# FFT plus mixture of experts on one core: the PSUM bank of the small sums becomes a second buffer for the second matmul's sums

## The chip, the cores and the metric

One core of a Trainium2 chip runs the whole kernel in one launch. The metric is the device time of that core in microseconds (us); lower is better. Three runs of the kernel before took 1113.00, 1111.27 and 1106.92 us, median 1111.27.

## The reference

```
X = np.fft.fft(x, axis=1)          # x: [8, 2496, 256] float32
X = np.fft.fft(X, axis=2)
t = X.real.reshape(19968, 256)
logits = t @ w_gate                # [256, 8]
e_idx  = argmax(logits);  gate_w = softmax(logits)[e_idx]
eom    = sigmoid(t @ w_output_gate)
h  = relu(t[rows of e] @ w1[e])    # w1: [8, 256, 1024]
ye = h @ w2[e]                     # w2: [8, 1024, 256]
out[rows of e] = gate_w * eom[:, e] * ye
```

Every one of the 19,968 tokens goes through one expert of eight, and which one is known only once its batch has been transformed.

## The kernel before, in words

**Transform.** The 8 batches are transformed one after another, in five steps each (`steps()`). `dstage` is the DFT along the features (its sums in a buffer of two PSUM banks, `psb_t`), `devac` splits its result into fp16 high and low parts (`ahi` on ACT, `alo` on DVE), `sstage` is the DFT along the sequence (again a `psb_t`), and `sevac` makes the finished rows. `gating` picks each token's expert on DVE, counts the tokens of each expert by two small matmuls (L592, L593) and has POOL scatter the rows to `scr` in device memory, sorted by expert.

**Experts.** The experts work on slots of 256 tokens. In each of three early rounds (as soon as 2, 4 and 6 batches are in `scr`) each expert gets two slots; a last round takes what is left after batch 8. `mm1` (L1134 on, its matmuls at L1146) makes 12 matmuls for one of a slot's four `hp` tiles (one PSUM bank each), ACT and DVE turn that into `hh` (L1150) and `hl` (L1151); `mm2` (matmuls at L1166) sums all four into one `yp` tile, which two ACT instructions scale into `y` (L1173, one for each 128 tokens), and POOL scatters `y` to the output.

**Weights.** SP loads the fp32 weights of an expert as four raw tiles (two halves of `w1`: `raw0b_134` and `raw0b_135`, two of `w2`: `raw1b_136` and `raw1b_137`), one buffer for each. In the first round a raw tile is first squared on ACT (`wsq`, L1107), which sums its energy; a matmul with ones adds that over the partitions (`wscale`, L369), and DVE makes a power of two of it (`p_w`, L276). ACT then converts the raw tile into an fp16 high part (`w0b` or `w1b`, L1126), DVE makes the low part (L1127), and only then can SP load the next expert's raw tile into that buffer (issued at L1095).

**Order.** `experts()` is the foreground and the transform steps of later batches are its background: the main loop takes one piece of the one, then as many of the other as its rates say. The order on SP and POOL is the order in which the program is written; on PE, ACT and DVE a scheduler picks it from the program and its buffers.

**PSUM.** There are eight banks. While early rounds and transform run together they hold two `hp`, one `yp`, two `psb_t` of two banks each, and one bank `psm_t` for all the small sums: the token counts (L592, L593), the energy of a batch (L455) and the weight energies (L369). From the last round on (pool `fpe2`) there are three `hp` and two `yp`. The pools of the first phase open again at the step FSTART, about 130 to 150 us into the span.

Of the kernel before, what the change touches and what calls it, by code (L numbers as in the profile page):

```python
# [11 lines left out]
F32 = mybir.dt.float32  # L12
# [221 lines left out]
def fft_moe_kernel(ctx: ExitStack, tc: tile.TileContext, xl, wg, w1, w2, tde, tdo, gt, ts0, tsm, tsr, tsq, cst, tid, out):  # L234
    nc = tc.nc
    PS = bass.MemoryType.PSUM
# [45 lines left out]
    if True:  # L282
        lp, xp, rp = ExitStack(), ExitStack(), ExitStack()
        pl = lambda st_, **kw: st_.enter_context(tc.tile_pool(reuse_waits="tile", **kw))
# [7 lines left out]
        pps = ExitStack()  # L292
        psb = pl(pps, name="psb", bufs=3, space=PS)
        psm = pl(pps, name="psm", bufs=2, space=PS)
        pool = {"b": psb, "m": psm}
# [59 lines left out]
        gate = {}  # L355
        smalls = {}

        def small():
            if "t" not in smalls:
                smalls["t"] = pool["m"].tile([128, 512], F32, name="psm_t", tag="m")  # L360
            return smalls["t"]

        wsrc = (w1, w2)
        wen = kp.tile([128, E, 2, 2], F32, name="wen")

        def wscale(e, m):
            ps = pool["m"].tile([128, 512], F32, name="psm_t", tag="m")[:, 0:1]
            for h in range(2):
                nc.tensor.matmul(ps, c_["ones"], wen[:, e, m, h:h + 1], start=(h == 0), stop=(h == 1))  # L369
            pow2_scale(pg, ps, 1, (7.0, 14.0)[m], "w", to=(wsc[:, m, e:e + 1], wiv[:, m, e:e + 1]))  # L370
            if m:
                nc.vector.tensor_mul(wsc[:, 2, e:e + 1], wiv[:, 0, e:e + 1], wiv[:, 1, e:e + 1])
# [180 lines left out]
        def gating(b):  # L553
# [11 lines left out]
            def t3(name, shape=(128, 20, 8)):  # L565
                return pg.tile(list(shape), F32, name="r_" + name, tag="r_" + name, bufs=1)

            m = t3("m", (128, 20))
# [19 lines left out]
            nc.vector.tensor_tensor_scan(inc.rearrange("p e j -> p (e j)"), c_["scanm"][P], oh.rearrange("p e j -> p (e j)"), 0.0, op0=ALU.mult, op1=ALU.add)  # L588
            yield
            yield "A"  # L590
            ps = pool["m"].tile([128, 512], F32, name="psm_t", tag="m")
            nc.tensor.matmul(ps[P, 0:8], c_["tri"][P], inc[:, :, 19], start=True, stop=True)  # L592
            nc.tensor.matmul(ps[:, 8:16], c_["ones"][P], inc[:, :, 19], start=True, stop=True)  # L593
            yield "C"
# [17 lines left out]
            t = t3("t", (128, 8, 20))  # L612
# [398 lines left out]
    if True:  # L1011
        fx = []
        psf = {}
# [51 lines left out]
        def scale_of(n, m):  # L1065
            rd, qi = sched[n][:2]
            return wsc[:, m, qi:qi + 1] if rd < LAST else ssc[:, m, qi:qi + 1] if rd == LAST else fbs[:, m, 0:1]
# [62 lines left out]
        def halves(a, h):  # L1130
            for k in ("hh", "hl"):
                a[k, h] = fx[0].tile([128, 4, 256], F16, name=k, tag=k, bufs=3)

        def mm1(n, g):  # L1134
            a = sl_[n]
            T = slice(0, a["N"])
            if g % 2 == 0:
                halves(a, g // 2)
            w1v = wbuf[a["wb"]][0][g // 2].rearrange("p a (k f) -> p a k f", k=2)
            ps = psf["h"].tile([128, 2, 256], F32, name="hp", tag="h", bufs=psf["hb"])  # L1140
            for k in range(2):
                f = 2 * g + k
                m = 0
                for kc in range(2):
                    for hl, x in ((0, kc), (0, 2 + kc), (1, kc)):
                        nc.tensor.matmul(ps[:, k, T], w1v[:, hl, kc, (f % 4) * 128:(f % 4 + 1) * 128], a["x"][:, x, T], start=(m == 0), stop=(m == 5))  # L1146
                        m += 1
            G = slice(2 * (g % 2), 2 * (g % 2) + 2)
            hh, hl = a["hh", g // 2], a["hl", g // 2]
            nc.scalar.activation(hh[:, G, T], ps[:, :, T], AF.Relu)  # L1150
            nc.vector.scalar_tensor_tensor(hl[:, G, T], ps[:, :, T], 0.0, hh[:, G, T], op0=ALU.max, op1=ALU.subtract)  # L1151

        def mm2(n, g):
            a = sl_[n]
            U, h = a["U"], g // 2
            M = min(128, a["N"])
            w2v = wbuf[a["wb"]][1][h].rearrange("p a (f d) -> p a f d", f=4)
            if g == 0:
                a["yp"] = psf["h"].tile([128, 2, 256], F32, name="yp", tag="y", bufs=psf["yb"])
                a["y"] = fx[0].tile([128, 2, 256], F32, name="y", tag="y", bufs=2)  # L1160
                a["ys"] = fx[0].tile([128, 2], F32, name="ysc", tag="ysc", bufs=2)
            u = g % 2 if U == 2 else 0
            for f in range(4) if U == 2 else range(2 * (g % 2), 2 * (g % 2) + 2):
                for m, (k, hl) in enumerate((("hh", 0), ("hh", 1), ("hl", 0))):

                    nc.tensor.matmul(a["yp"][0:M, u], a[k, h][:, f, u * 128:u * 128 + M], w2v[:, hl, f],  # L1166
                                     start=(g == 0 and f == 0 and m == 0), stop=(h == 1 and f == 3 and m == 2), skip_group_check=U == 2)
            ys = a["ys"]
            if g == 2:
                nc.vector.tensor_scalar(ys[:, 0:U], a["f"][:, 0:U, 0], scale_of(n, 2), None, op0=ALU.mult)  # L1170
            if g == 3:
                for u in range(U):
                    nc.scalar.activation(a["y"][0:M, u], a["yp"][0:M, u], AF.Copy, scale=ys[0:M, u:u + 1])  # L1173
                    put = nc.gpsimd.indirect_dma_start(  # L1174
                        out=out[:, :], out_offset=bass.IndirectOffsetOnAxis(ap=a["f"].bitcast(I32)[0:M, u, 1:2], axis=0),
                        in_=a["y"][0:M, u], in_offset=None, bounds_check=NTOK - 1, oob_is_err=False)
                    if sched[n][0] < FB:
                        free_order("out", put)
                del sl_[n]
# [114 lines left out]
    def background():  # L1294

        for m in steps_:
            yield C_STEP.get(m[0], C_END)
            if m[0] == "step":
                i, n = divmod(m[1], 5)
                for k, b in enumerate(BAS):  # L1300
                    if k and m[1] == 5 * b + 4:
                        for _ in table_a(k):
                            yield C_TAB
                    if m[1] == 5 * b + MARGIN:
                        ready.add(k)

                    if k and m[1] == 5 * b + 6 and k not in begun:
                        early(k, nc.sync.dma_start(fence, scr[DUM:DUM + 1, 0:1]))
        xp.close()
        for fill in (lambda: None, pads):  # L1310
            fill()
            while deferred:
                deferred.pop(0)()
                yield C_SCAT
        for _ in table_b():
            yield C_TAB
        pps.close()
        lp.close()
        fx.append(pl(ctx, name="fr2", bufs=2))
        psf["h"] = pl(ctx, name="fpe2", bufs=1, space=PS)  # L1320
        psf.update(hb=3, yb=2)
        add_raw(fx[1])
        add_wbuf(fx[1])
        ready.add(LAST)
# [9 lines left out]
    with tc.manual_schedule(engines=PH1):  # L1334
# [8 lines left out]
                break  # L1343
        pps.close()
        pps = ExitStack()
        psf["h"] = pl(ctx, name="fpe", bufs=1, space=PS)
        psf.update(hb=2, yb=1)
        pool["b"] = pl(pps, name="psb2", bufs=2, space=PS)
        pool["m"] = pl(pps, name="psm2", bufs=1, space=PS)
        next(fg)  # L1350
        load_x()
        bg = background()
# [44 lines left out]
```

## Time and profile before

| | |
|---|---|
| runs | 1113.00, 1111.27, 1106.92 us; median 1111.27 |
| profiled execution | 1110.9 us, its span 1109.0 us |
| granted TensorE clock, mean | 0.983 |
| PE busy | 1037.2 us, 94% of the span |
| ACT, DVE, POOL busy | 54%, 59%, 39% |
| matmuls recorded | 9866 |

The rows come from the trace of that one execution. A row of a timeline gives the start in us from the start of the span, the busy time, the engine, the line of the kernel, the operation, output<-inputs, the tile shapes, and how many like instructions stand in a row (x12); in square brackets is the idle time ahead of it and what ended that. A row of the waits says which instruction waited for which, how long in total, how many times, and the longest. A row of the chain is a piece of the chain of work that ended last. Names lack the buffer numbers in the trace and have them in the listings of the order.

### The profile page before, as it was taken

To read this page: it belongs to the slowest core of one execution; us is meant where nothing else is said; L and a number is where in the kernel's file an instruction comes from. 1 tells how busy PE (TensorE), PEld (TensorE's weight loads), DVE (VectorE), ACT (ScalarE), POOL (GpSimd) and SP (SyncE) were. 2 spreads that over 40 slices of the span, in tenths; PEclk is the share of its full clock that TensorE was granted. 3 is DMA by queue.
4 is the path that set the end of the run, shared out by engine and by line. 5 is a ranking of instruction groups with operands and counts; after the bars stand their busy time and mean duration, and the time that the engine had idled before them with its cause. 6 is when DMAs were issued, how large, how long until landed. Compare 5 with 4: busy or idle time off the path is not lost.

```text
span 1109.0 us, 27215 instructions
## 1 busy us (share of the span) xinstructions
PE 1037.2 (94%) x9866; PEld 928.0 (84%) x9866; DVE 654.5 (59%) x1352; ACT 599.6 (54%) x1095; POOL 434.5 (39%) x394
## 2 busy tenths in 40 slices
PE   5786679989899999999999999999999999999997
PEld 4675559878788999999998888888999989998996
DVE  6978646585577567557559454545355563555542
ACT  3765547665667456556554554554455553555542
POOL 0218835652675473346255772222221112212122
PEclk9998889999999999999999999999999999999999
DMA  9803465654546436466464786446556465665631
GB/s 353 308 19 115 151 171 153 180 166 130 157 133 194 123 104 167 119 158 164 137 166 122 204 208 171 144 105 181 135 138 183 127 183 133 156 180 144 170 87 28
DMA packets 152309, 170.97 MB, mean 154 GB/s; under 512 B 115309, under 2 KB 116207, under 8 KB 152164
## 3 DMA queue, kind: packets, MB, share of 16 engines
q1 hardware_dynamic: 136292, 126.48, 42.1%
q0 software_dynamic: 15728, 42.14, 11.4%
q8 instruction: 79, 1.29, 0.5%
q10 hardware_dynamic: 144, 0.52, 0.2%
q14 instruction: 66, 0.54, 0.2%
HBM read 149.51 MB, written 43.63 MB: 174 GB/s over the span
## 4 chain that ended last, share of the span: by engine, by line
PE 68%; DMA 11%; DVE 8%; ACT 5%; issue 4%; POOL 3%; SPq 1%; DVEq 0%; POOLq 0%; ACTq 0%
PE hp L1146 31%; PE yp L1166 30%; PE psb_t L516 4%; DMA raw1b<-in_w_dram 3%; DMA raw0b<-in_w_dram 3%; DMA out_dram<-y,xf 3%; PE psb_t L477 2%; DVE w0b L1127 2%; POOL scr L652 1%; ACT w1b L1126 1%; DMA scr<-rows,desti 1%; DVE w1b L1127 1%; POOL xt L408 1%; ACT w0b L1126 1%; ACT wsq L1107 1%
## 5 line engine op out<-in xcount | busy, mean ns | idle before, releaser
L1146 PE MATMUL hp<-xr,w0b 128*128 128x256 f16 (+2 forms) x4080 | 476.3, 267 | 10.5 <-DVE hl L1151 7.3
L1166 PE MATMUL yp<-w1b,hh 128*128 128x256 f16 x2560 | 437.6, 273 | 7.4 <-ACT y L1173 7.4
L1146 PEld LDWEIGHTS <-w0b 128*128 128x128 f16 x4080 | 381.1, 98 | 55.7 <-issue 8.2
L1174 POOL DMA_INDIRECT out_dram<-y,xf x160 | 187.4, 1171 | 542.4 <-ACT y L1173 501.8
L1166 PE MATMUL yp<-w1b,hl 128*128 128x256 f16 x1280 | 348.9, 273 | 0.0
L1151 DVE SCALAR_TENSOR_TENSOR hl<-hp,hh 128x512 f16<-128x512 f32 (+2 forms) x340 | 220.8, 654 | 204.5 <-ACT hh L1150 180.1
L1150 ACT ACTIVATE hh<-hp 128x512 f16<-128x512 f32 (+2 forms) x340 | 191.4, 566 | 234.9 <-PE hp L1146 231.1
L1166 PEld LDWEIGHTS <-hh 128*128 128x128 f16 x2560 | 248.6, 98 | 35.9 <-issue 8.2
L652 POOL DMA_INDIRECT scr<-rows,desti x160 | 174.3, 1089 | 76.8 <-issue 72.6
L1166 PEld LDWEIGHTS <-hl 128*128 128x128 f16 x1280 | 125.3, 98 | 14.4
L1173 ACT ACTIVATE y<-yp,ysc 128x256 f32<-128x256 f32 (+1 forms) x160 | 67.5, 469 | 45.0 <-PE yp L1166 40.4
L1127 DVE SCALAR_TENSOR_TENSOR w0b<-raw0b,wsc,w0b 128x1024 f16<-128x1024 f32 x44 | 60.7, 1379 | 49.4 <-ACT w0b L1126 49.4
L1127 DVE SCALAR_TENSOR_TENSOR w1b<-raw1b,wsc,w1b 128x1024 f16<-128x1024 f32 x44 | 56.3, 1281 | 42.4 <-ACT w1b L1126 41.6
L477 PE MATMUL psb_t<-tdet,ft 128*125 128x290 f32 (+1 forms) x200 | 61.1, 459 | 18.3 <-DVE ft L435 5.4
L477 PEld LDWEIGHTS psb_t<-tdet,ft 128*125 128x125 f32 (+1 forms) x200 | 40.7, 212 | 31.8 <-issue 9.6
L1126 ACT ACTIVATE w0b<-raw0b,wsc 128x1024 f16<-128x1024 f32 x44 | 50.3, 1145 | 30.2 <-PE hp L1146 29.2
L408 POOL TENSOR_TENSOR xt<-xt 128x500 f32<-128x500 f32 (+1 forms) x30 | 39.6, 1326 | 46.9 <-DMA xt<-in_xl_dram 32.9
L1126 ACT ACTIVATE w1b<-raw1b,wsc 128x1024 f16<-128x1024 f32 x44 | 50.3, 1145 | 13.0 <-PE yp L1166 13.0
L1127 DVE SCALAR_TENSOR_TENSOR w0b<-raw0b,ssc,w0b 128x1024 f16<-128x1024 f32 x32 | 40.8, 1282 | 22.5 <-ACT w0b L1126 21.6
L1127 DVE SCALAR_TENSOR_TENSOR w1b<-raw1b,ssc,w1b 128x1024 f16<-128x1024 f32 x32 | 41.1, 1283 | 21.9 <-ACT w1b L1126 21.0
L516 PE MATMUL psb_t<-ahi,tstq 125*128 125x145 f16 (+1 forms) x384 | 42.4, 229 | 2.2 <-DVE alo L490 2.2
L1126 ACT ACTIVATE w0b<-raw0b,ssc 128x1024 f16<-128x1024 f32 x32 | 36.3, 1144 | 14.7 <-DMA raw0b<-in_w_dram 13.6
(207 smaller groups left out, 950.8 us busy)
## 6 DMA issues: line engine op xcount, KB each, us to landing
raw0b<-in_w_dram SPq DMA_DIRECT2D x118, 512.0 KB
raw1b<-in_w_dram SPq DMA_DIRECT2D x118, 512.0 KB
xt<-in_xl_dram SPq DMA_DIRECT2D x40, 512.0 KB
scr<-rows,desti POOLq DMA_INDIRECT x160, 3.9
out_dram<-y,xf POOLq DMA_INDIRECT x160, 3.2
xr<-scr SPq DMA_TRANSPOSE x85
xf<-scr SPq DMA_DIRECT2D x75, 2.0 KB
tst<-in_ts_dram SPq DMA_DIRECT2D x2, 512.0 KB
```

Source lines behind the costliest of these rows:

```text
L408: eng.tensor_tensor(x0, x0, x1, op=ALU.add)
L477: nc.tensor.matmul(o[:, 0:290], ft[:, k, par, W], tdab[:, k], start=(k == 0), stop=(k == 1))
L516: nc.tensor.matmul(ps[:, k, c0:c0 + 145], tab[hl][t][K], a[K, kc, par, c0:c0 + 145], start=(n == 0), stop=(n == len(terms) - 1))
L652: free_order("scr", batch=b, inst=nc.gpsimd.indirect_dma_start(out=scr[:, :], out_offset=bass.IndirectOffsetOnAxis(ap=desti[:, j:j + 1], a ...
L1126: nc.scalar.activation(w[:, 0], r, AF.Copy, scale=sc)
L1127: nc.vector.scalar_tensor_tensor(w[:, 1], r, sc, w[:, 0], op0=ALU.mult, op1=ALU.subtract)
L1146: nc.tensor.matmul(ps[:, k, T], w1v[:, hl, kc, (f % 4) * 128:(f % 4 + 1) * 128], a["x"][:, x, T], start=(m == 0), stop=(m == 5))
L1150: nc.scalar.activation(hh[:, G, T], ps[:, :, T], AF.Relu)
L1151: nc.vector.scalar_tensor_tensor(hl[:, G, T], ps[:, :, T], 0.0, hh[:, G, T], op0=ALU.max, op1=ALU.subtract)
L1166: nc.tensor.matmul(a["yp"][0:M, u], a[k, h][:, f, u * 128:u * 128 + M], w2v[:, hl, f], start=(g == 0 and f == 0 and m == 0), stop=(h == 1 ...
L1173: nc.scalar.activation(a["y"][0:M, u], a["yp"][0:M, u], AF.Copy, scale=ys[0:M, u:u + 1])
L1174: put = nc.gpsimd.indirect_dma_start(out=out[:, :], out_offset=bass.IndirectOffsetOnAxis(ap=a["f"].bitcast(I32)[0:M, u, 1:2], axis=0), in_ ...
```

## The change

The early pools are laid out anew. `yp` gets a pool of its own with two banks (`fpy`), opened with the early rounds and kept to the end; `hp` keeps two banks, then three. There is no pool for the small sums any more (`pool["m"] = None`): the new function `few()` gives a small sum one bank of a `psb_t` buffer, of which there are two. So the 24 small-sum tiles made after the step FSTART (6 of the token counts, 4 of the batch energies, 14 of the weight energies) stand in line with `dstage` and `sstage` for those two buffers. No arithmetic is added or taken away. Every line from 358 on is numbered five higher in the changed kernel.

```diff
+        def few():
+            if pool["m"] is None:
+                return pool["b"].tile([128, 2, 512], F32, name="psb_t", tag="b")[:, 0]
+            return pool["m"].tile([128, 512], F32, name="psm_t", tag="m")
+
         def small():
             if "t" not in smalls:
-                smalls["t"] = pool["m"].tile([128, 512], F32, name="psm_t", tag="m")
+                smalls["t"] = few()
             return smalls["t"]
...
         def wscale(e, m):
-            ps = pool["m"].tile([128, 512], F32, name="psm_t", tag="m")[:, 0:1]
+            ps = few()[:, 0:1]
...
             yield "A"
-            ps = pool["m"].tile([128, 512], F32, name="psm_t", tag="m")
+            ps = few()
...
-            ps = psf["h"].tile([128, 2, 256], F32, name="hp", tag="h", bufs=psf["hb"])
+            ps = psf["h"].tile([128, 2, 256], F32, name="hp", tag="h")
...
-                a["yp"] = psf["h"].tile([128, 2, 256], F32, name="yp", tag="y", bufs=psf["yb"])
+                a["yp"] = psf["y"].tile([128, 2, 256], F32, name="yp", tag="y")
...
-        psf["h"] = pl(ctx, name="fpe2", bufs=1, space=PS)
-        psf.update(hb=3, yb=2)
+        psf["h"] = pl(ctx, name="fpe2", bufs=3, space=PS)
...
-        psf["h"] = pl(ctx, name="fpe", bufs=1, space=PS)
-        psf.update(hb=2, yb=1)
+        psf["y"] = pl(ctx, name="fpy", bufs=2, space=PS)
+        psf["h"] = pl(ctx, name="fpe", bufs=2, space=PS)
         pool["b"] = pl(pps, name="psb2", bufs=2, space=PS)
-        pool["m"] = pl(pps, name="psm2", bufs=1, space=PS)
+        pool["m"] = None
```

The scheduler answers to the new buffers with another order. SP's and POOL's orders are the same in both kernels. On PE, ACT and DVE the orders differ from about 130 us on and agree again from about 690 us. Three places matter below.

**Place A**, on ACT, about 168 to 188 us: the first round's second set of raw tiles. First as it is before:

```order
L1173 ACTIVATE y<-yp,ysc 128x256 x2
L1126 ACTIVATE w0b_139<-raw0b_135,wsc 128x1024
L1150 ACTIVATE hh<-hp 128x512
L1107 ACTIVATE wsq,wen<-raw0b_134 128x1024
...
L1126 ACTIVATE w1b_140<-raw1b_136,wsc 128x1024
L1107 ACTIVATE wsq,wen<-raw0b_135 128x1024
L1150 ACTIVATE hh<-hp 128x512
L446 ACTIVATE sq,en<-ft 128x4x125 x2
L1150 ACTIVATE hh<-hp 128x512
L1173 ACTIVATE y<-yp,ysc 128x256 x2
L1126 ACTIVATE w1b_141<-raw1b_137,wsc 128x1024
L1107 ACTIVATE wsq,wen<-raw1b_136 128x1024
```

And the same place with the change:

```order
L1178 ACTIVATE y<-yp,ysc 128x256 x2
L1112 ACTIVATE wsq,wen<-raw0b_134 128x1024
L1131 ACTIVATE w0b_139<-raw0b_135,wsc 128x1024
...
L1131 ACTIVATE w1b_140<-raw1b_136,wsc 128x1024
L1112 ACTIVATE wsq,wen<-raw0b_135 128x1024
L494 ACTIVATE ahi<-psb_t,p_x 125x580
L451 ACTIVATE sq,en<-ft 128x4x125 x2
L1112 ACTIVATE wsq,wen<-raw1b_136 128x1024
L1155 ACTIVATE hh<-hp 128x512 x2
L494 ACTIVATE ahi<-psb_t,p_x 125x580
L1178 ACTIVATE y<-yp,ysc 128x256 x2
L1131 ACTIVATE w1b_141<-raw1b_137,wsc 128x1024
```

The square of `raw0b_134` has moved ahead of the conversion of `raw0b_135`; the square of `raw1b_136` has moved ahead of two `hh`, the two `y` and the conversion of `raw1b_137`.

**Place C**, on ACT, about 212 to 218 us, one set of weights later. Before:

```order
L546 CAST rows<-rt 128x4x129
L1173 ACTIVATE y<-yp,ysc 128x256 x2
L1126 ACTIVATE w1b_141<-raw1b_137,wsc 128x1024
L1107 ACTIVATE wsq,wen<-raw1b_136 128x1024
L550 COPY rows<-rows 128x2x2x127
```

With the change:

```order
L551 CAST rows<-rt 128x4x129
L1112 ACTIVATE wsq,wen<-raw1b_136 128x1024
L1178 ACTIVATE y<-yp,ysc 128x256 x2
L1131 ACTIVATE w1b_141<-raw1b_137,wsc 128x1024
L555 COPY rows<-rows 128x2x2x127
```

Here too the square has moved ahead of the two `y` and the conversion.

**The start of the early rounds**, on PE, about 139 to 150 us (`tdet` and `ft` are the operands of `dstage`, `r_inc` and `wen` those of small sums). Before:

```order
L516 MATMUL psb_t<-ahi,tst_110 128x145
L477 MATMUL psb_t<-tdet,ft 125x290 x8
L592 MATMUL psm_t<-r_inc,cs 128x8
L593 MATMUL psm_t<-r_inc,cs 128x8
L369 MATMUL psm_t<-wen,cs 128x1 x2
L1146 LDWEIGHTS w0b_138
```

With the change:

```order
L521 MATMUL psb_t<-ahi,tst_110 128x145
L597 MATMUL psb_t<-r_inc,cs 128x8
L598 MATMUL psb_t<-r_inc,cs 128x8
L374 MATMUL psb_t<-wen,cs 128x1 x2
L521 LDWEIGHTS tst_110
L521 MATMUL psb_t<-ahi,tst_110 128x145
```

The eight `dstage` matmuls no longer stand between the transform and the first `hp`; they come later.

## Rows read from the trace of the kernel before

**Rows 1.** The first part of the page: busy time of each engine in us, share of the span, instructions.
```profile
PE 1037.2 (94%) x9866; PEld 928.0 (84%) x9866; DVE 654.5 (59%) x1352; ACT 599.6 (54%) x1095; POOL 434.5 (39%) x394
```

**Rows 2.** Busy time by stretch: the stretch and its length, then busy us and instructions of PE, PEld, DVE, ACT and POOL, the granted clock of PE (1.00 is the higher level), the DMA share and GB/s.
```profile
150.00:200.00 50.00, 49.54 (x434) 42.80 (x433) 26.30 (x56) 28.78 (x58) 23.55 (x24) 0.94 0.62 182
200.00:350.00 150.00, 134.52 (x1326) 121.30 (x1326) 102.08 (x238) 97.58 (x196) 85.21 (x77) 1.00 0.56 163
350.00:600.00 250.00, 250.00 (x2491) 228.90 (x2489) 158.17 (x359) 138.54 (x261) 120.91 (x107) 1.00 0.52 142
600.00:1109.00 509.00, 499.37 (x4810) 448.95 (x4808) 255.33 (x384) 250.48 (x399) 138.34 (x126) 1.00 0.55 147
```

**Rows 3.** What PE waited for between 200 and 350 us: total us, times, longest.
```profile
PE yp L1166 <- ACT y L1173: 7.4, 6, 2.5
PE hp L1146 <- DVE hl L1151: 5.3, 7, 1.5
```

**Rows 4.** What ACT waited for between 200 and 350 us: total us, times, longest.
```profile
ACT wsq L1107 <- DMA raw1b<-in_w_dram: 18.1, 9, 4.8
ACT wsq L1107 <- DMA raw0b<-in_w_dram: 15.5, 8, 4.5
...
ACT hh L1150 <- PE hp L1146: 1.7, 2, 0.9
```

**Rows 5.** A piece of the chain that ended last, from 205 to 280 us, and its first PE row after that: start, us, engine, what.
```profile
213.19 0.83 ACT y L1173 x2
214.02 1.04 ACT w1b L1126
215.09 1.30 DVE w1b L1127
216.41 4.10 DMA raw1b<-in_w_dram
...
347.89 1.47 PE hp L1146 x12
```

**Rows 6.** PE's timeline around 247 us.
```profile
247.61 0.38 PE L1166 MATMUL yp<-w1b,hh 128*128 128x256 f16 x2 [1.80 <-ACT y L1173]
...
250.89 1.36 PE L1146 MATMUL hp<-xr,w0b 128*128 128x256 f16 x11
```

**Rows 7.** ACT's timeline at place A.
```profile
168.87 1.15 ACT L1126 ACTIVATE w0b<-raw0b,wsc 128x1024 f16<-128x1024 f32 x1 [0.67 <-PE hp L1146]
...
170.41 1.05 ACT L1107 ACTIVATE wsq<-raw0b 128x1024 bf16<-128x1024 f32 x1
...
176.83 1.06 ACT L1107 ACTIVATE wsq<-raw0b 128x1024 bf16<-128x1024 f32 x1 [0.76 <-DMA raw0b<-in_w_dram]
177.88 0.58 ACT L1150 ACTIVATE hh<-hp 128x512 f16<-128x512 f32 x1
178.36 0.61 ACT L446 ACTIVATE sq<-ft 128x500 bf16<-128x500 f32 x1
...
179.71 0.58 ACT L1150 ACTIVATE hh<-hp 128x512 f16<-128x512 f32 x1
...
180.90 1.15 ACT L1126 ACTIVATE w1b<-raw1b,wsc 128x1024 f16<-128x1024 f32 x1
...
187.25 1.06 ACT L1107 ACTIVATE wsq<-raw1b 128x1024 bf16<-128x1024 f32 x1 [3.67 <-DMA raw1b<-in_w_dram]
```

**Rows 8.** SP's own queue: when it issued raw tiles' loads (two issues in the last row, from 178.40 to 183.73, so the second at 183.40).
```profile
166.31 0.33 SPq L1095 DMA_DIRECT2D raw0b<-in_w_dram  x1
...
172.79 0.33 SPq L1095 DMA_DIRECT2D raw0b<-in_w_dram  x1
...
178.40 5.33 SPq L1095 DMA_DIRECT2D raw1b<-in_w_dram  x2
```

**Rows 9.** ACT's timeline further on.
```profile
199.93 0.73 ACT L489 ACTIVATE ahi<-psb_t,p_x 125x580 f16<-125x580 f32 x1
...
206.15 0.61 ACT L446 ACTIVATE sq<-ft 128x500 bf16<-128x500 f32 x1
...
207.12 1.06 ACT L1107 ACTIVATE wsq<-raw0b 128x1024 bf16<-128x1024 f32 x1 [0.27 <-DMA raw0b<-in_w_dram]
...
215.59 1.06 ACT L1107 ACTIVATE wsq<-raw1b 128x1024 bf16<-128x1024 f32 x1 [0.53 <-DMA raw1b<-in_w_dram]
```

**Rows 10.** ACT's timeline between 236 and 250 us.
```profile
241.74 0.58 ACT L648 COPY rows<-r_car 128x8 int32<-128x8 int32 x5
...
245.68 1.06 ACT L1107 ACTIVATE wsq<-raw1b 128x1024 bf16<-128x1024 f32 x1 [1.94 <-DMA raw1b<-in_w_dram]
```

**Rows 11.** PE's timeline between 136 and 150 us.
```profile
139.14 2.20 PE L477 MATMUL psb_t<-tdet,ft 128*125 128x290 f32 x8 [1.50 <-DVE r_mx L582]
```

**Rows 12.** What PE waited for with a small sum's matmul between 140 and 200 us: total us, times, longest.
```profile
PE psm_t L369 <- DVE basem L610: 5.1, 1, 5.1
```

**Rows 13.** Two small sums on PE's timeline.
```profile
256.44 0.28 PE L455 MATMUL psm_t<-es,cs 128*128 128x1 f32 x2
...
261.75 0.51 PE L369 MATMUL psm_t<-wen,cs 128*128 128x1 f32 x4
```

**Rows 14.** The DVE instructions that read those two sums, on DVE's timeline.
```profile
260.52 0.15 DVE L276 TENSOR_SCALAR p_x<-psm_t 128x1 int32<-128x1 int32 x1
...
267.00 0.15 DVE L276 TENSOR_SCALAR p_w<-psm_t 128x1 int32<-128x1 int32 x1
```

## The prediction

> **What bounds the kernel now.** The page comes first: PE is busy for 94% of the span, DVE for 59%, ACT for 54% [rows 1]. That is an average, so the stretches come next [rows 2]. From 350 to 600 us PE is busy for 250.00 of 250 us, and from 600 us on for 499.37 of 509: there a PSUM buffer more or less buys nothing, because PE has work all the time. From 200 to 350 us it is busy for 134.52 of 150, so 15.5 us are idle, and the early layout of PSUM that the change touches is in force there. Any gain has to come out of those 15.5 us, and any loss there is carried to the end, since PE behind it has no idle time to catch up in.
>
> Third, what PE waits for in that stretch [rows 3]: `yp` for ACT's copy `y`, 7.4 us in six waits, and `hp` for DVE's `hl`, 5.3 us in seven. The first line is the wait that a second `yp` buffer takes away. The fourth view says whether that pays: the chain of work that ended last. From about 169 us to 347.89 us it has not one PE row; it runs through the loading of weights [rows 5]: ACT's `y` 0.83, ACT's conversion 1.04, DVE's low part 1.30, the raw tile's load 4.10, and so on to the first PE row at 347.89. A raw tile has one buffer, so its next load is issued only behind the low part, and ACT's next square waits for that load to land. ACT's waits say the same: 18.1 us for `raw1b` and 15.5 us for `raw0b` [rows 4], over twice PE's idle time. So the stretch is set by a loop of ACT, DVE and DMA for the weights, and PE's idle time is its shadow. What counts in this change is less what it takes from PE than what it does to ACT's order, since ACT executes in order and a square put ahead of a conversion makes the conversion wait for the square's load.
>
> **The waits for `yp`: worth nothing here.** Take the largest kind: at 247.61 PE had waited 1.80 us for `y` [rows 6]. Had it not, it would have come to the `hp` matmuls at 250.89 sooner, and stood there, for their buffer is freed by an `hl` that follows an `hh` on ACT, in a queue behind the square that began only at 245.68 [rows 10]. The idle time changes its name. I take 0; the other end is all 7.4 us, kept for the range as a rival. The Trainium skill (Perfetto Trace Analysis, Optimization Strategy under Identifying Performance Opportunities) says that gaps repeating on the engine that should be saturated can mean too little PSUM for the next tile; by that rule the sum would gain the 7.4 us. The chain without a PE row speaks against it here.
>
> **Place A, +4.0 us.** These are two moves on ACT. (1) The square of `raw0b_134` now stands ahead of the conversion of `raw0b_135`. Its load was issued at 166.31 [rows 8] and had landed when the square started, 170.41 [rows 7]. The conversion, which began at 168.87, now begins behind that square at 170.41 + 1.05 = 171.5; with 1.15 for itself and 1.30 for the low part [rows 5] the buffer is free at 173.9, against a load issued at 172.79: 1.1 us later. That load landed just before the square at 176.83, so now that square starts at 177.9 and ends at 179.0. (2) Behind it now come one `ahi` (0.73, the row at 199.93 [rows 9]), two `sq` (1.35, from 178.36 to 179.71 [rows 7]) and the square of `raw1b_136` (1.06), and only then the `hh` that before started at 177.88: it starts at 182.1, 4.2 us later. Then two `hh` at 0.48 apart, one `ahi` at 0.73 and two `y` at 0.71 lead to the conversion of `raw1b_137` at 184.5 to 185.0, against 180.90. Its next load was issued at 183.40 and its square, which waited 3.67 us for it, began at 187.25; both move by 3.6 to 4.2. I take 4.0. The low end is 1.1, if only the load of the first move is carried; the high end is 4.6, if the second `hh` must also wait for its matmuls.
>
> **Place B, +0.7 us.** At 206.15 a `sq` filled ACT's wait for a load that ended at 207.12 [rows 9]. In the new order the `sq` comes behind that square, so its 0.6 to 0.8 us stand on the path to the next conversion. Low end 0.
>
> **Place C, +3.5 us.** Before, two `y` and the conversion ran from 213.19 to 215.06 [rows 5], while the load for the next square was on its way, and the square began at 215.59 when it had landed [rows 9]. Now the square comes first: the two `y` begin behind it, at 215.59 + 1.06 = 216.65, and the conversion at 217.45 instead of 213.92 (it overlaps the second `y`): 3.5 us. It is on the chain, and its low part releases the load issued at 216.41, which takes 4.10. Low end 0, if by then the load is no longer what the loop waits for; high end 3.5.
>
> **Place D, +0.5 us.** Five copies of 0.1 us each at 241.74 now stand behind a square that waited 1.94 us for its load and began at 245.68 [rows 10]: what was hidden in that wait is now behind it. Low end 0.
>
> **Given back, −0.8 us.** In the same stretch ACT waited twice, 1.7 us in all, at `hh` for PE's `hp` [rows 4]. With ACT late these shrink; I take one of the two off. Ends 0 and 1.7.
>
> **The rest, 0.** Eight `dstage` matmuls that filled 2.20 us of an idle PE [rows 11] now run later, within PE's 15.5 idle us. The wait of 5.1 us at a small sum at 142 us goes, since it has another buffer [rows 12], but the first `hp` waits for scattered rows anyway and not for this. A small sum now holds a `psb_t` buffer until DVE has read it: from 256.44 to 260.52 and from 261.75 to 267.00 in the two that I followed [rows 13, 14], 4.1 and 5.3 us, with `dstage` waiting for that buffer. PE is off the chain there, so I take 0; the trace of before has no such wait, so its ends are 0 and, if it lands on the loop once, the difference between the hold and the 2 to 3 us of other PE work, 1.5 to 3 us. That such a hold delays `ahi` and with it a later conversion is the last rival.
>
> **Sum.** 4.0 + 0.7 + 3.5 + 0.5 − 0.8 = 7.9 us. On the profiled execution's 1110.9 us that makes 1118.8, say **1119.0 us**. That execution is 0.4 us below the median of the three runs, 1111.27, so nothing is corrected for it. About 0.5% (5.6 us) is what a measurement of this kernel can tell from no change; slower by that begins at 1116.8, faster ends at 1105.7.
>
> **The rivals.**
>
> *The lag is swallowed: 1111 us.* ACT's 33.6 us of waits for loads [rows 4] belong to two pairs of raw buffers, and a delay of one pair counts only while that pair is the later one. If at A and C the other pair sets the pace, each +4 is taken up by a shorter wait at the next square. For it: raw0b and raw1b wait about alike, 15.5 and 18.1 us. Against it: ACT is one queue, and place C is on the chain itself [rows 5]. With only the low ends of the terms the sum is 1.1 − 1.7, or some 1110; with A alone 4.0 − 0.8, or 1114. Both cannot be told from no change. That the change does nothing at all, because the scheduler's order makes up for it, ends here too.
>
> *Faster: the waits for `yp` were the bound: 1103.5 us.* PE cannot begin the next slot's `mm2` until ACT has read the last one, and when ACT stands in a wait for a load, PE stands with it. With two buffers PE goes on and the `hl` it then needs may be there already. It gives 1110.9 − 7.4 = 1103.5. It decides if PE, freed of these six waits, does not block at `hp` within the next 2 us. For it: it is the first line of PE's waits [rows 3]. Against it: `hp` is the second line with 5.3 us, and no PE row is in the chain.
>
> *Slower still, by the holds: 1124 us.* The 14 weight sums belong to the first round, and so mostly to the stretch before 350 us. If two of them hold back a `dstage` by 1.5 to 3 us while its `ahi` and the `sq` behind it stand ahead of a conversion in ACT's queue, 5 us come on top of 7.9.
>
> **How the numbers follow.** The forecast (the lag is carried) has 0.52: each term is read from rows, but the walk holds PE's and DVE's orders fixed. The swallowed lag has 0.33, the gain 0.11, the holds 0.04. The forecast's own range, from the low end of A and C to the high end of all, is about 1114 to 1123; below 1116.8 I put 0.02 of its 0.52, and those count as no change. So faster 0.11, the same 0.35, slower 0.54. The range leaves out the gain and half of the holds and takes in the rest: 1107 to 1124.
>
> **What would show it.** Right: PE's line `yp` for `y` is nearly gone between 200 and 350 us; PE's idle time there is about 23 us instead of 15.5, most of it at `hp` for `hl` or for weights; the chain through that stretch is still ACT, DVE and loads without PE; the conversion of `raw1b` near 181 starts near 185, the one near 214 starts 7 or 8 us later than before, and everything behind 350 us is later by that while its busy time stays. Place A is wrong if that first conversion is within 1 us of before; place C if the lag does not grow between 190 and 222 us. If PE's idle time in the stretch falls to about 8 us and the span with it, the `yp` waits were the bound. If a new line `psb_t` for `p_w` or `p_x` of more than 3 us appears among PE's waits, the holds count. If PE has idle time behind 350 us where there was none, a part that I held for full is not, and the sum is wrong in a place I did not price.

## The result, and the profile after

The changed kernel took 1116.51 us in the median of its runs, the kernel before 1111.26 on the same chip. The ratio is 1.0054, with a 95% interval of 1.0031 to 1.0078: 6.0 us slower, between 3.4 and 8.7. The forecast was 7.9 us slower, 1119.0 us.

One thing must be known before the rows are read. The runs of the changed kernel lie between 1110.67 and 1120.31 us (one disturbed run apart), and the profiled execution is the shortest, 1110.67; that of before took 1110.9, near its median. So this trace shows what became of each step, but not the whole loss. A second trace of the changed kernel, further down, is from an execution at its median, on another chip.

Busy time by stretch, in the columns of [rows 2], in the first trace of the changed kernel:

```profile
150.00:200.00 50.00, 49.98 (x435) 43.27 (x434) 24.34 (x49) 28.24 (x52) 23.07 (x23) 0.98 0.59 176
200.00:350.00 150.00, 136.31 (x1312) 121.00 (x1310) 100.47 (x232) 96.66 (x193) 86.89 (x78) 0.98 0.55 162
```

PE idles for 13.7 us between 200 and 350 (17.7 in the second trace), not for the 23 that I expected, and from 350 on it is as full as before. What PE and ACT waited for between 200 and 350 us (total, times, longest; answers to [rows 3, 4]):

```profile
PE hp L1151 <- DVE hl L1156: 10.9, 11, 2.6
PE psb_t L521 <- DVE alo L495: 2.6, 2, 2.0
```

```profile
ACT wsq L1112 <- DMA raw1b<-in_w_dram: 19.3, 8, 4.7
ACT wsq L1112 <- DMA raw0b<-in_w_dram: 17.7, 9, 4.3
```

The 7.4 us of waits for `yp` are gone, and the waits for `hp` have doubled, from 5.3 to 10.9: most of that idle time did change its name. ACT waits for loads a little longer, 37.0 us against 33.6. Now places A and C on ACT's timeline, answers to [rows 7, 9]:

```profile
166.86 1.06 ACT L1112 ACTIVATE wsq<-raw0b 128x1024 bf16<-128x1024 f32 x1 [1.73 <-DMA raw0b<-in_w_dram]
...
167.91 1.13 ACT L1131 ACTIVATE w0b<-raw0b,wsc 128x1024 f16<-128x1024 f32 x1
...
178.23 1.06 ACT L1112 ACTIVATE wsq<-raw1b 128x1024 bf16<-128x1024 f32 x1 [0.55 <-DMA raw1b<-in_w_dram]
...
181.57 1.17 ACT L1131 ACTIVATE w1b<-raw1b,wsc 128x1024 f16<-128x1024 f32 x1
...
187.99 1.06 ACT L1112 ACTIVATE wsq<-raw1b 128x1024 bf16<-128x1024 f32 x1 [4.76 <-DMA raw1b<-in_w_dram]
...
216.21 1.06 ACT L1112 ACTIVATE wsq<-raw1b 128x1024 bf16<-128x1024 f32 x1 [1.32 <-DMA raw1b<-in_w_dram]
...
217.27 0.82 ACT L1178 ACTIVATE y<-yp,ysc 128x256 f32<-128x256 f32 x2
217.98 1.14 ACT L1131 ACTIVATE w1b<-raw1b,wsc 128x1024 f16<-128x1024 f32 x1
```

These must be read against where the early rounds began: the first `hp` matmul is at 146.62 here and at 149.87 in the trace of before. At 181.57 the conversion is only 0.7 us later than before (180.90), but 3.9 later counted from the first `hp`; its square at 187.99 stands 4.0 later in the same count. At C the square, at 216.21, is 0.6 us later than before (215.59 [rows 9]) and the conversion, at 217.98, 4.0 us later than in the chain of before (214.02 [rows 5]), so C has added 3.4. Counted so, both are what the walk through the order gave: 4.0 and 3.5.

Two things must be held against this. Without that count the conversion at 181.57 is within 1 us of before, which is what I had named as the sign that place A is wrong. And the count holds more than the order of the squares. From the first `hp` to this conversion it is 31.0 and 30.0 us in two traces of the kernel before, 35.0 and 35.9 in two of the changed kernel, but 32.5 in the changed kernel with the squares put back in the old order (set 1). By these traces 2.4 to 3.4 us at A are the order's.

At the start there is a wait that I had not seen coming (PE, 120 to 150 us):

```profile
PE psb_t L597 <- DVE r_inc L593: 8.4, 1, 8.4
PE hp L1151 <- DMA xr<-scr: 2.8, 1, 2.8
```

The token counts' small sum now stands in the middle of the sequence DFT, and PE stands with it for 8.4 us. The second row says that it costs nothing there: when it is over, the first `hp` still waits for its rows.

### The profile page after: what moved, and what is told of

Same layout as the page of the kernel before. It is cut to its first block, busy times and chain, and to the rows that moved or that the text cites. A ratio compares the mean times of both kernels' runs of the same rounds, so it can differ in the third digit from the quotient of the medians.

```text
span 1108.9 us, 27205 instructions
## 1 busy us (share of the span) xinstructions
PE 1038.5 (94%) x9866; PEld 928.8 (84%) x9866; DVE 657.0 (59%) x1352; ACT 600.0 (54%) x1095; POOL 432.0 (39%) x394
## 5 line engine op out<-in xcount | busy, mean ns | idle before, releaser
L1132 DVE SCALAR_TENSOR_TENSOR w1b<-raw1b,ssc,w1b 128x1024 f16<-128x1024 f32 x32 | 41.1, 1283 | 22.2 <-ACT w1b L1131 20.5
L1132 DVE SCALAR_TENSOR_TENSOR w0b<-raw0b,ssc,w0b 128x1024 f16<-128x1024 f32 x32 | 40.8, 1283 | 22.2 <-ACT w0b L1131 21.5
```

What stands on the lines that cost most here:

```text
L1132: nc.vector.scalar_tensor_tensor(w[:, 1], r, sc, w[:, 0], op0=ALU.mult, op1=ALU.subtract)
```

## The experiments

All times are for whole runs; "us" of a ratio is its distance from 1 times the median of before on that chip (1140.09, 1151.55 and 1112.30 us in the three sets).

**Set 1: is it the order, or the small sums?**

The changed kernel unaltered.

> The changed kernel unaltered, for a second trace beside the first, whose execution took 1110.67 us, the shortest of its fast ones (median 1116.5). Theory (squares ahead of conversions on ACT): an execution near 1116 shows PE's hp matmuls 4 us late against before by about 194 us and 6 to 8 us late by 266 us, counted from the first hp, which starts within 1 us of before's 149.87 and not 3.25 us earlier as in the first trace. Rival (the token counts' small sum, placed in the middle of the sequence DFT, idles PE for 8.4 us at 130 us, the clock falls and stays low): the extra time of such an execution stands in a granted clock below 0.9 somewhere between 150 and 260 us, with PE busy there.

Ratio 1.0047 (1.0019 to 1.0074), 5.4 us. The trace comes from an execution of 1147.11 us, the median being 1147.05. The first `hp` is at 147.5, so 2.3 us earlier than in the trace of before and not within 1 us; counted from it, the `hp` matmul that before starts at 194 us is 4.9 us late and the one at 266 us 9.3, more than I expected. The chain of work that ended last, in this trace, a piece of it:

```profile
195.77 1.29 DVE w0b L1132
197.08 4.12 DMA raw0b<-in_w_dram
201.22 1.15 ACT wsq L1112 x2
...
211.48 1.05 ACT w1b L1131
212.55 1.30 DVE w1b L1132
213.87 4.09 DMA raw1b<-in_w_dram
```

It is the loop of [rows 5] again: low part, load, square, conversion. The granted clock is 0.99 in both stretches of the first rows, 150 to 200 and 200 to 350 us, but not everywhere in them:

```profile
240.00:250.00 10.00, 7.31 (x54) 5.85 (x54) 8.97 (x21) 5.42 (x12) 8.55 (x8) 0.83 0.71 170
```

That is a clock below 0.9, but for 10 us only and with PE idle for 2.7 of them, nearly all in one wait for `hl`. After the 7.2 us of PE idle time at the start of this trace the clock is 0.96 from 150 to 160 us and 1.00 from there to 240. The rival's clock that stays low isn't there.

The kernel before with three squares put ahead of conversions, by an edge that orders the issue on ACT and waits for nothing else:

```diff
-            nc.scalar.activation(sq, raw[0][m][h], AF.Square, accum_out=wen[:, e, m, h:h + 1])
+            i_ = nc.scalar.activation(sq, raw[0][m][h], AF.Square, accum_out=wen[:, e, m, h:h + 1])
+            if (n, m, h) in ((4, 0, 0), (4, 1, 0), (6, 1, 0)):
+                tc.add_manual_dep(cv[n - 2, m, 1], getattr(i_, "ins", i_).name,
+                                  mybir.DependencyInfo(mybir.DependencyClass.NoSync, mybir.DependencyReason.DATA), reason="square first")
```

(`cv` holds the conversion of each slot and half.)

> The kernel before with its own PSUM layout, and three squares put ahead of conversions on ACT as the changed kernel has them: at place A (raw0b_134 ahead of w0b_139, raw1b_136 ahead of w1b_141) and at place C (raw1b_136 ahead of w1b_141). Theory: +4.0 at A and +3.5 at C less what is given back, so 1115 to 1119 us. Rival (small sums and the PE idle time at 130 us): within 2 us of before, 1109 to 1113.

Ratio 1.0088 (1.0061 to 1.0115): 10.0 us, 7.0 to 13.1. The order alone, on the old layout, gives the loss and more; 4 to 8 us were expected. The edge names three squares, but the scheduler answered with more: between 170 and 220 us several pieces on each of ACT, PE and DVE stand elsewhere than in the kernel before, twelve `hp` matmuls and the next conversion among them. So the 10.0 us are the price of that whole order.

The changed kernel with the same three squares put behind the conversions:

```diff
+            back = cv.get((n - 2, m, 1)) if (n, m, h) in ((4, 0, 0), (4, 1, 0), (6, 1, 0)) else None
+            with tc.issue_after(back) if back is not None else nullcontext():
                 nc.scalar.activation(sq, raw[0][m][h], AF.Square, accum_out=wen[:, e, m, h:h + 1])
```

> The changed kernel with the same three squares put back behind the conversions, as before has them; PSUM layout and small sums as changed. Theory: the 5 to 6 us go, 1109 to 1112 us, perhaps a little less, since the waits for yp are gone too. Rival (small sums): stays at 1115 to 1118.

Ratio 0.9986 (0.9966 to 1.0006), 1139.22 us where the changed kernel took 1147.05 on the same chip. The loss is gone, with the small sums where the change put them and with their 7.2 us of PE idle at the start:

```profile
PE psb_t L597 <- DVE r_inc L593: 7.2, 1, 7.2
```

So the loss is the order's, and the small sums are not its cause.

The small sums moved, `yp` left with one buffer:

```diff
-        psf["y"] = pl(ctx, name="fpy", bufs=2, space=PS)
+        psf["y"] = pl(ctx, name="fpy", bufs=1, space=PS)
...
         psf["h"] = pl(ctx, name="fpe2", bufs=3, space=PS)
+        psf["y"] = pl(ctx, name="fpy2", bufs=2, space=PS)
```

> The small sums take a transform buffer, but yp keeps one buffer until the last round (one PSUM bank lies unused). Its scheduler order has the small sum of the token counts in the middle of the sequence DFT, the square of raw1b_136 behind the conversion at A, and ahead of it at C. Theory: about half of the loss, +2 to +4, so 1113 to 1115 us, with waits for yp back at about 7 us. Rival (small sums carry the loss): the whole of it or more, 1116 to 1120.

Ratio 1.0060 (1.0040 to 1.0080), 6.8 us: a miss, as much as the whole change where I expected half. Taken alone it speaks for the rival; with the run before it, it can't, and with the squares put behind the conversions this very layout is faster than the kernel before (0.9964, the last run of set 3). What it has of the order is the first move of A and the move at C, and it lacks the second `yp` buffer. The next sets size both moves.

**Set 2: which place, and what the squares cost in the other sets of weights.**

Two of the three edges, and then the third alone:

```diff
-            if (n, m, h) in ((4, 0, 0), (4, 1, 0), (6, 1, 0)):
+            if (n, m, h) in ((4, 0, 0), (4, 1, 0)):
```

> The kernel before with only the two squares of place A put ahead of conversions (raw0b_134 ahead of w0b_139, raw1b_136 ahead of w1b_141). Theory: +4 us at 180 us, carried to the end: ratio 1.003 to 1.006. Rival (what counts is place C, and the load swallows place A): ratio 0.999 to 1.001.

Ratio 1.0062 (1.0039 to 1.0086): 7.1 us, 4.5 to 9.9. A alone is above the 4.0 of the forecast. Here too the scheduler moved other pieces between 170 and 220 us, the same as with all three edges, so the 7.1 are not the two squares' alone.

> The kernel before with only the square of raw1b_136 of place C put ahead of the conversion w1b_141 (but not ahead of the two y); PE's order is not changed at all. Theory: the conversion starts behind the square at 216.65 instead of 213.92, so +2.7 us, carried: ratio 1.0015 to 1.004. Rival (only A counts, or the waits for loads swallow it): 0.999 to 1.001.

Ratio 1.0008 (0.9978 to 1.0037): −2.5 to +4.3 us, which holds both numbers. This edit moves the one conversion on ACT and nothing on PE. On ACT the step is there:

```profile
211.81 0.83 ACT L1177 ACTIVATE y<-yp,ysc 128x256 f32<-128x256 f32 x2
...
214.43 1.06 ACT L1107 ACTIVATE wsq<-raw1b 128x1024 bf16<-128x1024 f32 x1 [1.79 <-DMA raw1b<-in_w_dram]
...
215.49 1.13 ACT L1129 ACTIVATE w1b<-raw1b,wsc 128x1024 f16<-128x1024 f32 x1
```

The conversion that would have followed `y` at 212.5 starts at 215.5, behind the square and its wait. In this trace those 3 us are still there at 427 us (the table further down); whether they reach the end of the run stays open.

Then the rule for every expert of the first round, on the changed kernel and on the kernel before, since both have squares ahead of conversions in later sets of weights:

```diff
-            back = cv.get((n - 2, m, 1)) if (n, m, h) in ((4, 0, 0), (4, 1, 0), (6, 1, 0)) else None
+            back = cv.get((n - 2, m, 1)) if h == 0 else None
```

> The changed kernel with the rule for every expert of the first round: the square of a first raw half never ahead of the conversion of the second half of the set before. In the later sets both kernels have such squares ahead. Theory: as with the old order at A and C, and 1 to 4 us less, if the later ones cost something too: ratio 0.994 to 0.999. Rival (from 260 us on PE's own work sets the pace): the same as with the old order, 0.998 to 1.000.

Ratio 0.9925 (0.9899 to 0.9952): 8.6 us faster than before, 5.5 to 11.6, twice what I gave it. This version beats both kernels.

> The kernel before with that rule for every expert of the first round, PSUM as before. Theory: the same 1 to 4 us less than before, 0.996 to 1.000; against the changed kernel with the rule it shows what the second yp buffer is worth once the order is equal: 0 to 2 us. Rival: 1.000.

Ratio 0.9950 (0.9923 to 0.9977): 5.8 us faster, a little more than the 4 that I gave it. What PE and ACT waited for between 200 and 350 us in this last one, with one `yp` buffer as in the kernel before:

```profile
PE hp L1149 <- DVE hl L1154: 2.7, 3, 2.1
PE yp L1169 <- issue: 1.0, 3, 0.4
PE hp L1149 <- DVE eo L540: 1.0, 1, 1.0
PE yp L1169 <- ACT y L1176: 0.9, 2, 0.7
```

```profile
ACT wsq L1109 <- DMA raw0b<-in_w_dram: 11.5, 6, 2.9
ACT wsq L1109 <- DMA raw1b<-in_w_dram: 10.7, 5, 3.4
```

ACT's waits for loads fall from 33.6 to 22.2 us, and PE's waits for `yp` from 7.4 to 0.9, without a buffer added. PE waited for `y` because `y` stood behind a square, and the square behind a load.

**Set 3: the first move of A by itself, and what else the bank is good for.**

The kernel before, unaltered, for a trace from the chip of this set.

> The kernel before, unaltered, for a trace from the same chip as the three others of this call. Theory: first hp at 148 to 150 us; hp matmul 336 (of 4080) at 243 to 247 us, some 6 us earlier than in the traces with squares ahead at place A (250.4 to 252.7 us). On a chip that takes 1140 to 1150 us: PE waits for nothing but its own issue between 500 and 720 us, so that stretch has nothing to do with the change. Rival: hp 336 at 250 us here too, and the difference of the earlier traces was one of chips.

1109.77 us; the first `hp` is at 148.1 and the 337th `hp` matmul at 242.9, as in the first trace of before (244.2).

The first move of A alone:

```diff
-            if (n, m, h) in ((4, 0, 0), (4, 1, 0), (6, 1, 0)):
+            if (n, m, h) in ((4, 0, 0),):
```

> The kernel before with only the first move of place A: the square of raw0b_134 ahead of the conversion w0b_139. As the prediction priced it, 1.1 us of the 4.0 at A: ratio 1.000 to 1.002. Rival (this move sets off most of A, since everything on ACT behind it waits for the load too): 1.003 to 1.006.

Ratio 1.0029 (1.0009 to 1.0050): 3.2 us, 1.0 to 5.6, where 1.1 was priced, just inside the interval. The two traces of this set side by side, the kernel before first:

```profile
166.18 1.15 ACT L1126 ACTIVATE w0b<-raw0b,wsc 128x1024 f16<-128x1024 f32 x1 [1.08 <-PE hp L1146]
...
168.42 1.06 ACT L1107 ACTIVATE wsq<-raw0b 128x1024 bf16<-128x1024 f32 x1 [0.61 <-DMA raw0b<-in_w_dram]
```

```profile
169.88 1.06 ACT L1107 ACTIVATE wsq<-raw0b 128x1024 bf16<-128x1024 f32 x1 [1.60 <-DMA raw0b<-in_w_dram]
...
170.94 1.14 ACT L1129 ACTIVATE w0b<-raw0b,wsc 128x1024 f16<-128x1024 f32 x1
```

The conversion is 4.8 us later, of which 1.4 were there already at the conversion ahead of it (161.65 and 163.06): 3.4 are the move's. Before, ACT converted while the load was under way; now it waits 1.6 us for the load and then squares for 1.06. The buffer's next load, which the low part of that conversion releases, is issued here by SP, before and then with the move:

```profile
169.68 0.33 SPq L1095 DMA_DIRECT2D raw0b<-in_w_dram  x1
```

```profile
173.42 0.33 SPq L1095 DMA_DIRECT2D raw0b<-in_w_dram  x1
```

It is 3.7 us later, of which 1.4 were there at the load before it too (164.14 and 165.54): 2.3 are the move's, where the forecast had 1.1.

The bank as a third `hp` buffer, the small sums in turn with `hp`, and the rule for the squares:

```diff
-            return pool["b"].tile([128, 2, 512], F32, name="psb_t", tag="b")[:, 0]
+            return psf["h"].tile([128, 512], F32, name="psm_t", tag="h")
...
-        psf["y"] = pl(ctx, name="fpy", bufs=2, space=PS)
-        psf["h"] = pl(ctx, name="fpe", bufs=2, space=PS)
+        psf["y"] = pl(ctx, name="fpy", bufs=1, space=PS)
+        psf["h"] = pl(ctx, name="fpe", bufs=3, space=PS)
...
-        psf["h"] = pl(ctx, name="fpe2", bufs=3, space=PS)
+        psf["y"] = pl(ctx, name="fpy2", bufs=2, space=PS)
```

> The bank of the small sums becomes a third hp buffer instead of a second yp buffer, the small sums take turns with hp, and no square stands ahead of a conversion in the first round. PE's waits for hp are 5 to 11 us between 200 and 350 us in all traces so far. Theory (ACT and the loads set the pace there): no better than before with late squares, 0.994 to 0.998. Rival (hp buffers are the next limit): 0.990 to 0.993.

Ratio 0.9913 (0.9883 to 0.9943): 9.7 us faster than before. That is in the rival's range, but its interval reaches into the theory's, and it can't be told from the second `yp` buffer with the same rule (0.9925, on another chip).

The small sums moved, one `yp` buffer, and the rule:

> The small sums take a transform buffer, yp keeps one, and no square stands ahead of a conversion in the first round: beside before with late squares (0.9950) it tells what the small sums' place costs, beside the change with late squares (0.9925) what the second yp buffer brings, at equal rule of order. Theory: small sums cost nothing, 0.994 to 0.996. Rival (they hold back the transform): 0.998 to 1.003.

Ratio 0.9964 (0.9944 to 0.9984), just over the theory's end. Beside 0.9950 with the small sums in their own bank that is 1.6 us more, within the intervals of both; the rival's 0.998 is hardly inside. On the same chip, and with the same rule, the version with the third `hp` buffer took 1104.77 us against 1108.15 here, and the two intervals do not overlap: the bank is worth about 3 us there (the small sums stand elsewhere too).

## Why the prediction was right, and where its sum was not

The direction, the mechanism and the total were right: 7.9 us forecast, 6.0 measured (5.4 on a second chip). The loss comes and goes with the order of the squares on ACT. The single terms are less sure than the total: the first move of A was sized too small, C is not resolved in a run's time, and the 0 for `yp` was followed at one wait of six only. How the traces move, in one table: the time in us at which the n-th of the 4080 `hp` matmuls starts, and the time from the 385th to the 433rd.

```
                                      1st    145th  337th  385th..433rd  913th
kernel before                        149.9   184.5  244.2      21.3      424.5
changed, first trace                 146.6   185.2  250.7      17.3      427.6
set 1: changed, second trace         147.5   187.0  252.7      17.9      432.8
set 1: changed, old order            148.2   186.2  247.0      18.4      428.9
set 1: order alone                   150.0   188.8  252.7      21.1      432.4
set 1: small sums alone              147.6   188.1  252.3      22.0      432.4
set 2: A alone                       149.5   185.4  250.4      21.2      430.4
set 2: C alone                       148.5   183.2  246.5      20.3      427.4
set 3: before again                  148.1   181.8  242.9      22.2      422.3
set 3: first move of A               149.6   187.1  248.2      21.0      428.0
```

Only rows of one layout should be set against each other, since the changed layout has other matmuls between the `hp`: with the old order its 913th is 4.4 us later than in before, and that kernel is not slower.

- *What bounds the kernel: right.* In the second trace of the changed kernel the chain is ACT, DVE and loads up to 294 us, where PE enters it for some 10 us; and putting conversions ahead of squares, with no buffer added, takes 5.8 us off the kernel before.
- *The signs named ahead: some came, some not.* The line `yp` for `y` is gone, and no line `psb_t` for `p_w` or `p_x` appears. PE's idle time is 13.7 and 17.7 us and not 23. The conversion near 181 is 0.7 us later than before by the clock of the first trace and 2.5 in the second, not 4, and the one near 214 is 4.1 and 5.9 later, not 7 or 8. In part this is the start: the first `hp` of these two traces comes 3.3 and 2.3 us earlier than in that of before, which the forecast had at 0.
- *Place A: mechanism right, the first move sized too small.* 1.1 us forecast, 2.3 measured at the next load, 3.2 (1.0 to 5.6) in the run. The walk itself holds: on set 3's trace of before it puts the conversion behind the square, 168.42 + 1.06, 3.3 us later (3.4 measured), and with 1.15 and 1.30 the next load at 171.9 and not at 169.68, 2.3 later. In the first trace it gave 1.1 because there the old order's low part took 2.71 us, while the new order's was priced at 1.30:

```profile
170.06 2.71 DVE L1127 SCALAR_TENSOR_TENSOR w0b<-raw0b,wsc,w0b 128x1024 f16<-128x1024 f32 x1 [0.95 <-ACT w0b L1126]
```

So the size was that of one execution. The whole of A was forecast at 4.0: the run of A alone says 7.1 (4.5 to 9.9), with other pieces moved as well, and the traces say 2.4 to 3.4 for the order in the changed kernel. Which of these the changed kernel pays at A stays open.

- *Place C: seen on ACT, 3.4 us in the first trace and 3.0 in its own run's.* Counted from the first `hp`, its own trace is 3 to 4 us behind the two traces of before at the 337th matmul and 4 to 5 at the 913th; in the run's time it is not resolved (−2.5 to +4.3).
- *Place B:* in the first trace the square is 1.0 us later than before and the conversion behind it, at 209.77, 1.6: 0.6 added, against 0.7. Place D was not tried.
- *The waits for `yp`, taken at 0: right at the place I followed, open for the rest.* I followed one wait, at 247.61, as the largest; by [rows 3] the longest was 2.5 us, and it was another. At the place I followed the walk holds. In the changed kernel with the old order PE doesn't wait for `y` there, and at the `hp` matmuls that before come at 250.89 it waits for `hl` instead (1.02 us in the second trace of the changed kernel, 0.13 in the first):

```profile
252.89 1.70 PE L1154 MATMUL hp<-xr,w0b 128*128 128x256 f16 x12 [2.08 <-DVE hl L1159]
```

The longest wait of before is this one; with two buffers it is gone, and PE does go on:

```profile
280.20 0.38 PE L1166 MATMUL yp<-w1b,hh 128*128 128x256 f16 x2 [2.52 <-ACT y L1173]
```

In the table the 48 matmuls from the 385th on take 20.3 to 22.2 us in all seven traces with one `yp` buffer and without the rule for the squares, and 17.3 to 18.4 in the three with two buffers. That is 3 to 4 us, but with two buffers 48 `yp` matmuls stand among them and with one 60, and twelve of these take 1.31 us; so some 2 us are PE's idle time given back there. (With the rule it is 17.8 and 18.5 with one buffer, 17.1 with two: the late squares take the same wait away.) Over the stretch from 200 to 350 us nothing is left of it. PE in the kernel before on set 3's chip, and in the changed kernel with the old order:

```profile
200.00:350.00 150.00, 138.27 (x1336) 124.07 (x1335) 102.00 (x242) 96.85 (x197) 82.97 (x75) 0.98 0.57 165
```

```profile
200.00:350.00 150.00, 134.80 (x1312) 120.54 (x1310) 99.94 (x231) 94.96 (x190) 86.02 (x77) 0.99 0.57 158
```

It idles for 11.7 and, in the first trace, 15.5 us before, and for 15.2 with the second buffer, with waits for `hl` of 11.0 us where the first trace of before had 5.3. In whole runs the sign is a gain each time and resolved never: −1.6 us (−3.9 to +0.7) with the change in the old order; 0.9925 against 0.9950 with the rule; 5.4 us with the change against 10.0 with the order alone, and of these 4.6 us the two traces show 3.8 as idle time of PE between 500 and 720 us (13.8 and 17.6), far from any of the six waits. By the Trainium skill (Perfetto Trace Analysis, Optimization Strategy) such gaps can mean too little PSUM for the next tile; here the waits went away with the second buffer, and PE's idle time in the stretch did not.

- *Why the total came out:* in part by luck. The order alone costs 10.0 us (7.0 to 13.1) where 7.5 were forecast for these three moves, and A and C by themselves add up to 8.0. What holds the changed kernel at 6.0, whether a second `yp` buffer worth some 3 us, the earlier start or a smaller A, these runs can't tell apart.
- *The range:* its low end of 1114 does not follow from the terms; with A and C at their low ends the sum is 1.5 us, which gives 1112.4. Nothing measured hangs on it.
- *The start, priced at 0, holds a small lead.* The first `hp` comes at 146.3 to 149.3 in the seven traces with the small sums moved and at 148.1 to 150.0 in the seven with their own bank, 1.5 us earlier in the mean. This was not tested by itself, and it spreads by 3 us between executions; in the first trace of the changed kernel it is 3.25 and hides much of the loss.
- *The rivals:* the swallowed lag fell with the order alone (10.0 us) and A alone; the holds fell with the changed kernel in the old order; the gain by `yp` fell with the result, for the waits went and the kernel became slower.

What stays open: how large A is in the changed kernel, whether C reaches the end of the run, what the second `yp` buffer is worth, and how much of the runs' spread (10 us for the changed kernel, 7 for before) comes from the start.

## What to carry to other kernels

When a change of buffers lets a scheduler choose a new order, look first at where instructions that wait for a load have moved on an engine that executes in order: one square ahead of one conversion cost about 3 us (1.0 to 5.6), and the right order, with no buffer added, gained 5.8 us where the second `yp` buffer gained nothing that the runs resolve. Walk a new order through more than one trace of the old one: the same walk gave 1.1 us on one execution's rows and 2.3 on another's. And follow the waits of a group one by one, the longest first, before calling them a shadow; then look at the idle time of the whole stretch, since what is given back at one wait can be lost again at the next.

## What had not been expected of the hardware

On two of the other chips all variants took about 30 to 40 us longer, and most of that time lies in one stretch, in which PE on the first chip is busy for 220.00 of 220 us with and without the change. PE in the second trace of the changed kernel, and in the trace of before of the third set, between 500 and 720 us:

```profile
500.00:720.00 220.00, 206.21 (x1891) 179.14 (x1890) 122.42 (x269) 104.69 (x184) 106.12 (x94) 0.97 0.57 151
```

```profile
500.00:720.00 220.00, 220.00 (x2096) 197.86 (x2095) 133.02 (x283) 115.69 (x200) 110.25 (x98) 1.00 0.62 165
```

In the first of them PE makes 1891 matmuls in that time and in the second 2096, and 11.6 of its 13.8 idle us wait for nothing but its own issue. What this issue waits for, the traces don't show. Hence ratios were taken within one chip only, and even there this idle time differs from trace to trace (11.8 to 17.6 us in set 1).

The clock also fell at one short idle time. In both traces of the changed kernel twelve `hp` matmuls that take 1.47 us [rows 5] took 2.74 after PE had waited 2.65 us; in the first trace this is a stretch with a mean granted clock of 0.66, so part of it at the lower level:

```profile
241.37 2.74 PE L1151 MATMUL hp<-xr,w0b 128*128 128x256 f16 x12 [2.65 <-DVE hl L1156]
```

```profile
240.00:245.00 5.00, 3.63 (x21) 2.70 (x22) 5.00 (x16) 1.81 (x5) 4.54 (x4) 0.66 0.74 190
```
